# Batch 0's second part in nine transfers to tiles of their own, and two more raw buffers for the first sixteen weight loads

## The chip, the cores and the metric

The kernel runs on one core of one Trainium2 chip. The metric is the device time of one execution in microseconds. Five engines work in parallel, each through its own instructions in a fixed order: PE (matmul, with PEld for its weight loads), DVE, ACT and POOL (elementwise work), and SP, which here only issues DMA transfers. Who must wait for whom is settled by semaphores.

## The reference

Three layers follow one another. In the attention, for each of 4 batches and 8 heads (576 rows, 64 columns), a causal softmax of q and k is applied to v, and mixed with a memory read-out.

```python
scores = np.where(causal, -1000000000.0, scale * q @ k.T)
a = softmax(scores); local = a @ v
mem_out = (phi(q) @ M_prev) / (phi(q) @ z_prev + 1e-6)      # phi(x) = elu(x) + 1
attn = g * mem_out + (1 - g) * local                         # g = sigmoid(beta) by head
h = x @ moe_w_in;  y = (h * sigmoid(h)) @ moe_w_out          # 512 -> 2048 -> 512
g = y @ w_gate;    out = (silu(g) * (y @ w_val)) @ w_out     # 512 -> 1536 -> 512
```

## The kernel before

The weights are 64-bit numbers, so each tile of them is loaded as raw integers (`raw8`, 512 KB), decoded to float32 by ACT (L731) and DVE (L732, L733), and split by ACT and POOL (L214, L773) into a high and a low half, `w`. The attention works on pairs of heads. Batch 0 is done in two parts: part A takes rows 0 to 255 for all four pairs (phase "A"), part B rows 256 to 575 (phase "B"); the later batches follow pair by pair. As soon as part A is done, the first MoE layer starts on it: matmuls `h` (L870) with four raw tiles of the first weights, the gate (`th`, `gh`, `gl`), then matmuls `y` (L928) with four raw tiles of the second weights. The layer is cut into four weight slices, in the order `A0 A1 B1 B0 A2 B2 A3 B3` of part and slice; `w` tiles are also stored to DRAM (`wd`, L796) and fetched again later. A generator interleaves MoE matmuls and attention steps, and a scheduler then fixes each engine's order before the program runs, by times that it estimates. What stands in an engine's order is not changed by the hardware.

One pair of part B is this chain: transposes of q and k (`psq`, `psk`, L367), evacuation to `Q` and `kT` on ACT (L220), six score products (`pss`, L434 and L509), each with a minimum on DVE (L486, L510), five exponentials on ACT, the normalisation (`r` on DVE, `s` on POOL, L523), transposes of the result (`pst`), their evacuation (`tb`), and the product with v (`U`, L619), which gives `x` for the MoE layer. The memory read-out runs beside it (`e`, `qp`, `psm`, `n`, `mr`). The attention's products share five PSUM banks, so PE can start the next product only when DVE or ACT has emptied a bank.

In part B each pair's rows are loaded into one `q_t` and one `k_t` and one of two `v_t`; the next pair's q and k follow when the transposes of this pair are through (`lq`), and v when the pair is done (`lv`). `Prep` holds the raw weight tiles: three buffers, loaded two ahead:

```python
            self.done[key] = self.split(t, key)
            self.prefetch(ahead)
            for d, t in self.post:
                nc.sync.dma_start(out=d, in_=t)
```

Of the kernel before, what the change touches and what calls it, by code (L numbers as in the profile page):

```python
# [8 lines left out]
F32 = mybir.dt.float32  # L9
# [4 lines left out]
I32 = mybir.dt.int32  # L14
# [3 lines left out]
P = 128  # L18
BIG = 1.0e9
CFG = dict(  # L20
    raw8=3,
    raw=3,
    g=1,
    th=2,
    ps_m=3,
    ps_a=dict(A=5, B=5, G=5),
    ps_s=dict(),
    run=3000,
# [3 lines left out]
    rows=1,  # L32
# [14 lines left out]
    ahead=2,  # L47
# [18 lines left out]
    n_rows=2,  # L66
    n_s4=dict(A=0, B=2, F=2, G=1),
    lb=3,
    bufsA={'*': 4},
    bufsB={'*': 2},  # L70
    bufsF={'*': 2},
# [22 lines left out]
def kernel(  # L94
# [15 lines left out]
    nc = tc.nc  # L110
    B, H, S, D = q.shape
# [4 lines left out]
    NP = H // 2  # L116
    NT = B * S
    SA = 256
# [10 lines left out]
    def f(ap):  # L129
        return ap.bitcast(F32)  # L130
# [20 lines left out]
    kp = kept.enter_context(tc.tile_pool(name="kp", bufs=1))  # L151
    pha = ExitStack()
    rawp = pha.enter_context(tc.tile_pool(name="rawp", bufs=CFG["raw"], side="right"))
    cur, ph2 = {"raw": rawp}, {}
# [72 lines left out]
    rows, bds = {}, []  # L227
# [14 lines left out]
            q4s.append(t)  # L242

    q4s, gate = [], []
    rowsA = {}
    units = []

    def bd_of(u):
# [3 lines left out]
    def load_bd(b, eng):  # L252
        t = bds[b % 2]
        for hh in range(2):
            r = slice(64 * hh, 64 * hh + 64)
            eng.dma_start(
                out=t[r, :, 64 * hh:64 * hh + 64], in_=M_prev[b].rearrange("(p c) d e -> c d p e", c=2)[hh]
            )
            with nc.allow_non_contiguous_dma(reason="one number of each row"):
                eng.dma_start(out=t[r, :, P + hh], in_=z_prev[b].rearrange("(p c) d -> c d p", c=2)[hh])  # L260

    def load_A():
        for nm in "qkv":
            rowsA[nm] = cur["pool"].tile([P, 2, H, D], F32, name=nm + "A")

        def go(nm, h, eng):
            src = {"q": q, "k": k, "v": v}[nm]
            for c in range(2):
                eng.dma_start(
                    out=rowsA[nm][:, c, h], in_=src[0, h, P * c:P * c + P, :].rearrange("h p d -> p h d")  # L270
                )

        go("q", slice(0, 2), nc.sync)
        go("k", slice(0, 2), nc.scalar)
        go("q", slice(2, 4), nc.sync)
        go("k", slice(2, 4), nc.scalar)
        go("q", slice(4, 8), nc.sync)
        go("k", slice(4, 8), nc.sync)
        nc.sync.dma_start(out=bt, in_=beta.rearrange("(o h) -> o h", o=1).broadcast_to([P, H]))
        load_bd(0, nc.sync)  # L280
        go("v", slice(0, 8), nc.sync)

    owner = {}

    def rows_of(u):
        return rows[u % len(rows)]

    def load_rows(u, names):
        b, p, sups = units[u]
        t = rows_of(u)  # L290
        for nm in names:
            owner[nm, u % len(rows) if nm == "v" else 0] = u
            src = {"q": q, "k": k, "v": v}[nm]
            c0 = 0 if nm == "v" or 0 in sups else 2
            for hh in range(2):
                x = src[b, 2 * p + hh]
                nc.sync.dma_start(
                    out=t[nm][:, c0:4, hh, :], in_=x[P * c0:512, :].rearrange("(c p) d -> p c d", p=P)
                )
            x = src[b, 2 * p:2 * p + 2]  # L300
            if nm == "v":
                nc.sync.dma_start(out=t[nm][0:64, 4], in_=x[:, 512:S].rearrange("h p d -> p h d"))
            else:
                nc.sync.dma_start(out=t[nm][:, 4], in_=x[:, S - P:S].rearrange("h p d -> p h d"))
# [41 lines left out]
    def unit(u):  # L346
        b, p, sups = units[u]
        o = {}
        ph = "A" if sups == (0,) else "B" if sups == (1,) else "F" if b < CFG["stackb"] else "G"
# [4 lines left out]
        hs2 = slice(2 * p, 2 * p + 2)  # L354
# [2 lines left out]
            return CFG.get(ph, {}).get(key, CFG[key])  # L357

        def own(nm):
            assert ph == "A" or owner[nm, u % len(rows) if nm == "v" else 0] == u, (nm, u)  # L360

        def row_of(nm, c):
            return rowsA[nm][:, c, hs2] if ph == "A" else rows_of(u)[nm][:, c]

        def T(dst, src, start=True):
            n = src.shape[0]
# [2 lines left out]
        def transposed(nm, sup, out, e, scale):  # L369

            own(nm)
            ps = cur["ps_a"].tile([P, 512], F32, tag="a", name="ps" + nm)
            n = (SA, SB)[sup]
            for i, c in enumerate(BLK[sup]):
                x = P * i if c < 4 else n - P
                T(ps[:, x:x + P], row_of(nm, c).rearrange("p h d -> p (h d)"))
            cps(e, out, ps[:, 0:n], scale)
# [215 lines left out]

        def AV():
            own("v")
            Us = {}
            for sup in sups[::-1]:
# [32 lines left out]

        def nxt_load(names):
            w = u + (len(rows) if names == "v" else 1)
            if ph != "A" and w < len(units) and w >= NP:
                load_rows(w, names)

        def nxt_bd():
# [39 lines left out]
    slots, ready, at_slot = {}, {}, 0  # L676
    for u, key in enumerate(units):
        step, stages = unit(u)
# [14 lines left out]
    NSLOT = max(slots) + 1  # L693

    def load_B():
        for u in range(NP, NP + len(rows)):
            load_rows(u, "qkv" if u == NP else "v")

    slots[1].insert(0, setup_beta)
    slots[CFG["lb"]].append(load_B)  # L700
    slots[CFG["lb"]].append(lambda: load_bd(1, nc.sync))

    def attn_slot(s):
        for st in slots[s]:
# [2 lines left out]

    w1 = {}

    def load64(w, j, part, after=None):  # L710

        raw = cur["raw"].tile([P, 512, 2], I32, tag="raw8", name="raw8", bufs=CFG["raw8"])
        w2 = w.bitcast(I32)
        if after is not None:
            nc.gpsimd.tensor_copy(raw.bitcast(F32)[:, 0, 0:1], f(after))
        if part == 0:
            nc.sync.dma_start(
                out=raw.rearrange("p (k n) t -> p k (n t)", k=KD),
                in_=w2[:, 2 * P * j:2 * P * (j + 1)].rearrange("(k p) n -> p k n", p=P),
            )  # L720
        else:
            nc.sync.dma_start(out=raw.rearrange("p n t -> p (n t)"), in_=w2[P * j:P * j + P, :])
        return raw

    def decode(raw, t=None):
        hi, lo = raw[:, :, 1], raw[:, :, 0]
        u = hi.bitcast(F32)
        if t is None:
            t = cur["raw"].tile([P, 512], F32, tag="raw", name="raw", bufs=CFG["raw"])
        ti = t.bitcast(I32)  # L730
        nc.scalar.activation(out=t, in_=u, func=ACTF.Prelu, scale=2.0**-111, alpha=-(2.0**32))  # L731
        nc.vector.tensor_single_scalar(ti, ti, 3, op=ALU.logical_shift_left)  # L732
        nc.vector.scalar_tensor_tensor(ti, lo, 29, ti, ALU.logical_shift_right, ALU.bitwise_or)  # L733
        return t

    seen = {}

    def r_(ap):
        return ap.bitcast(F32R)

    def raw_w1(*key):
        if key in seen:
            return None
        if key[0] == 0:
            return load64(w1_in, key[1], 0)
        raw = cur["raw"].tile([P, 512, 2], I32, tag="raw8", name="raw8", bufs=CFG["raw8"])
        _, s, e = key
        nc.sync.dma_start(
            out=raw.rearrange("p (j n) t -> p j (n t)", j=NW),
            in_=w1_out.bitcast(I32)[P * NW * s:P * NW * (s + 1), 2 * P * e:2 * P * (e + 1)].rearrange(  # L750
                "(j p) n -> p j n", p=P
            ),
        )
        return raw

    def split_w1(t, key):
        if key in seen:
            w = wp.tile([P, 2, 512], F32, tag="w", name="w")
            nc.sync.dma_start(out=w, in_=seen[key])
            return r_(w[:, 0]), r_(w[:, 1])  # L760
        w = split_wp(decode(t), "1")
        seen[key] = dram.tile([P, 2, 512], F32, name="wd%d_%d" % (key[0], len(seen)))
        prep1.post.append((seen[key], w))
        return r_(w[:, 0]), r_(w[:, 1])

    def split_wp(t, kind):
        w = wp.tile([P, 2, 512], F32, tag="w", name="w")
        split_to(r_(w[:, 0]), r_(w[:, 1]), t, kind)
        return w
# [5 lines left out]
    class Prep:  # L775
# [9 lines left out]
                key = self.todo.pop(0)  # L785
                self.raws.append((key, self.load(*key)))

        def step(self, ahead=CFG["ahead"]):
            self.prefetch(1)
            if not self.raws:  # L790
                return
            key, t = self.raws.pop(0)
            self.done[key] = self.split(t, key)
            self.prefetch(ahead)
            for d, t in self.post:
                nc.sync.dma_start(out=d, in_=t)  # L796
            self.post = []

        def need(self, key):
            while key not in self.done:  # L800
# [3 lines left out]


    prep1 = Prep(raw_w1, split_w1)

    def token_block(key):
# [594 lines left out]
    if True:  # L1403
        open_at("atA")
        setup_attn()
        load_A()
        setup()
        items = moe1()
# [7 lines left out]
        for sg in segs:  # L1416
            r = sg["r"]
# [5 lines left out]
        for kind, val in items:  # L1423
# [7 lines left out]
            else:  # L1431
# [3 lines left out]
                if goals:  # L1435
                    x = (cost - c0) / (goals[0][0] - c0)
# [20 lines left out]
        with tc.manual_schedule(engines={mybir.EngineType.PE}):  # L1457
            for n, (kind, i, x, y) in enumerate(pos):
# [3 lines left out]
                else:  # L1462
                    down(i, x, y)
                    k = x * NJ2 + y
# [38 lines left out]
```

## Time and profile before

| what | value |
|---|---|
| median of 3 runs | 1058.24 us (1055.73 to 1062.23) |
| the profiled execution | 1061.61 us, its span 1059.8 us |
| PE busy | 1035.1 us (98% of the span) |
| DVE, ACT, POOL busy | 647.3, 539.8, 394.6 us |
| granted TensorE clock, mean | 0.993 |
| bytes moved by DMA | 258.16 MB, mean 244 GB/s |

The span runs from the first to the last instruction; the profiled execution's own time is 1.8 us more. Busy shares are means over stages with different limits: from 660 us on PE alone sets the time, and the change stands in the first 110 us.

### The profile page before, as it was taken

The numbers are of one execution on the slowest core, as the hardware profiler recorded it, in microseconds if no ns is written. First come the engines' busy times: TensorE is split into PE (matmuls) and PEld (weight loads), VectorE is DVE, ScalarE is ACT, GpSimd is POOL, SyncE is SP. The second block draws the span as 40 slices with busy tenths as digits, with TensorE's granted clock in tenths as the row PEclk, the third lists the DMA queues.
The fourth block names the chain that finished last, engine by engine and source line by source line (L and its number), as shares of the span: only waits on it lengthen the run. The fifth ranks groups of instructions, "written<-read, shape, count | busy, mean of one in ns | idle before, by whom it ended". The sixth has DMA issues, their size and how long they took to land.

```text
span 1059.8 us, 18826 instructions
## 1 busy us (share of the span) xinstructions
PE 1035.1 (98%) x6622; PEld 953.2 (90%) x6622; DVE 647.3 (61%) x1521; ACT 539.8 (51%) x1259; POOL 394.6 (37%) x463
## 2 busy tenths in 40 slices
PE   7799999999999999999999999999999999999998
PEld 5577988888878899888999899999999999999998
DVE  6796767886545644765245553566845669356573
ACT  6684877866656655675454441333613336133351
POOL 4684644678656647552579651000000000000000
PEclk9899999999999999999999999999999999999999
DMA  8995766478977569762299866777987778777784
GB/s 195 321 301 156 253 222 200 119 236 266 297 254 260 183 203 365 254 200 74 100 313 308 336 238 229 251 258 249 339 261 265 250 250 285 255 268 246 250 286 147
DMA packets 168670, 258.16 MB, mean 244 GB/s; under 512 B 76800, under 2 KB 113152, under 8 KB 168576
## 3 DMA queue, kind: packets, MB, share of 16 engines
q1 hardware_dynamic: 167488, 256.70, 73.3%
q8 instruction: 53, 0.87, 0.3%
q10 hardware_dynamic: 1088, 0.26, 0.1%
q14 instruction: 41, 0.34, 0.1%
HBM read 197.67 MB, written 59.24 MB: 242 GB/s over the span
## 4 chain that ended last, share of the span: by engine, by line
PE 79%; DVE 6%; POOL 4%; DMA 4%; ACT 4%; issue 3%; SPq 0%; POOLq 0%; ACTq 0%; DVEq 0%
PE y L928 14%; PE h L870 13%; PE oac L1207 11%; PE gb L1207 11%; PE po L1314 9%; PE pb L1314 4%; PE U L619 4%; PE gd L1207 4%; PE pss L434 3%; PE pst L367 3%; PE psm L445 1%; DMA raw<-in_moe_w_out_dram 1%; DMA raw<-in_moe_w_gate_dram 1%; POOL wo L996 1%; DVE raw L733 1%
## 5 line engine op out<-in xcount | busy, mean ns | idle before, releaser
L870 PE MATMUL h<-x,w 128*128 128x432 f32 (+2 forms) x1152 | 226.4, 346 | 4.4 <-ACT w L214 3.0
L870 PEld LDWEIGHTS h<-x,w 128*128 128x128 f32 x1152 | 196.6, 190 | 16.5 <-ACT w L214 3.2
L928 PE MATMUL y<-gh,w 128*128 128x432 f32 (+2 forms) x768 | 166.3, 349 | 2.7 <-DVE th L878 1.6
L928 PEld LDWEIGHTS y<-gh,w 128*128 128x128 f32 x768 | 131.6, 190 | 14.5 <-issue 3.5
L880 POOL TENSOR_TENSOR gl<-th,gh 128x432 fp32r<-128x432 f32 (+2 forms) x96 | 105.5, 1102 | 78.7 <-ACT gh L214 63.9
L1207 PE MATMUL gb<-yT,w 128*128 128x384 f32 x648 | 124.8, 336 | 0.0
L1207 PEld LDWEIGHTS gb<-yT,w 128*128 128x128 f32 x648 | 113.1, 188 | 0.0
L878 DVE SCALAR_TENSOR_TENSOR th<-th,h 128x432 f32<-128x432 f32 (+2 forms) x96 | 52.5, 550 | 80.7 <-ACT th L877 80.6
L523 POOL TENSOR_TENSOR s<-s,r 128x128 f32<-128x128 f32 (+4 forms) x96 | 68.4, 740 | 74.5 <-DVE r L540 19.8
L1314 PE MATMUL po<-w,ph 128*128 128x256 f32 x516 | 93.8, 283 | 0.0
L928 PE MATMUL y<-gl,w 128*128 128x432 f32 (+2 forms) x384 | 88.5, 344 | 0.6 <-POOL gl L880 0.6
L490 ACT ACTIVATE s<-s,mn 128x128 f32<-128x128 f32 (+3 forms) x128 | 70.9, 555 | 22.6 <-DVE mn L486 21.2
L1207 PE MATMUL oac<-yB,w 128*128 128x384 f32 x432 | 81.3, 336 | 0.0
L1314 PEld LDWEIGHTS po<-w,ph 128*128 128x128 f32 x516 | 81.2, 191 | 0.0
L732 DVE TENSOR_SCALAR raw<-raw 128x512 int32<-128x512 int32 x68 | 42.0, 618 | 62.6 <-ACT raw L731 62.3
L1279 ACT CAST ph<-r 128x384 fp32r<-128x384 f32 x108 | 51.0, 513 | 56.0 <-DVE r L1233 35.7
L1207 PEld LDWEIGHTS oac<-yB,w 128*128 128x128 f32 x432 | 75.4, 188 | 0.0
L1314 PE MATMUL po<-w,pl 128*128 128x256 f32 x258 | 73.0, 283 | 0.0
L928 PEld LDWEIGHTS y<-gl,w 128*128 128x128 f32 x384 | 67.6, 190 | 4.3 <-POOL gl L880 1.5
L214 ACT CAST gh<-th 128x432 fp32r<-128x432 f32 (+2 forms) x96 | 49.1, 513 | 42.8 <-DVE th L878 31.5
L731 ACT ACTIVATE raw<-raw 128x512 f32<-128x512 f32 x68 | 45.5, 669 | 48.1 <-DMA raw<-in_moe_w_gate_dram 17.3
L1280 DVE TENSOR_TENSOR pl<-r,ph 128x384 fp32r<-128x384 f32 x108 | 55.9, 554 | 17.8 <-ACT ph L1279 17.1
(163 smaller groups left out, 1999.5 us busy)
## 6 DMA issues: line engine op xcount, KB each, us to landing
w<-wg SPq DMA_DIRECT2D x108, 512.0 KB, 4.7
w<-wd SPq DMA_DIRECT2D x80, 512.0 KB, 5.5
wg<-wo SPq DMA_DIRECT2D x36, 512.0 KB, 3.6
w<-woT SPq DMA_DIRECT2D x36, 512.0 KB, 4.9
wd<-w SPq DMA_DIRECT2D x32, 512.0 KB, 4.2
raw<-in_moe_w_out_dram SPq DMA_DIRECT2D x28, 512.0 KB, 5.5
w<-woB SPq DMA_DIRECT2D x27, 512.0 KB, 4.8
w<-wg SPq DMA_DIRECT2D x36, 256.0 KB, 4.8
```

Source lines behind the costliest of these rows:

```text
L214: nc.scalar.copy(out, in_)
L490: nc.scalar.activation(out=a, in_=a, func=ACTF.Exp, scale=-1.0, bias=mn, accum_out=o["sm", sup][:, col:col + 1])
L523: nc.gpsimd.tensor_mul(a, a, r.to_broadcast([P, w]))
L731: nc.scalar.activation(out=t, in_=u, func=ACTF.Prelu, scale=2.0**-111, alpha=-(2.0**32))
L870: nc.tensor.matmul(ps[:, :nt], w[:, kk, :], x[:, kk, :nt], start=(m == 0), stop=(m == 3 * KD - 1))
L878: nc.vector.scalar_tensor_tensor(th[:, :nt], th[:, :nt], 1.0, ps[:, :nt], ALU.add, ALU.mult)
L880: tt(CFG["gl" if n >= CFG["n0"] else "gl0"]).tensor_sub(gl[:, :nt], th[:, :nt], f(gh[:, :nt]))
L928: nc.tensor.matmul(ps[:, :nt], w[:, c], g[:, :nt], start=(m == 0), stop=(m == last))
L1207: nc.tensor.matmul(dst, w[wi][:, P * kk:P * kk + P], y[ny][:, yi, kk], start=(start and m == 0), stop=(stop and m == 5), skip_group_check= ...
L1279: nc.scalar.copy(ph, src)
L1280: nc.vector.tensor_sub(pl, src, f(ph))
L1314: nc.tensor.matmul(dst, a[:, c], x, start=(begin and m == 0 and own_bank), stop=(end and m == 2), skip_group_check=True,)
```

## The change

Rows 256 to 575 of q, k and v of batch 0 are loaded for all four pairs at once, by three transfers each, into `qB`, `kB` and `vB`, which nothing overwrites. The first two row blocks of v come from part A's `vA`, which now lives on through part B. So phase B has no row loads of its own, and the loads of batch 1's first pair have nothing to wait for. Of the first sixteen raw tiles, numbers 2, 4, 7, 9, 12 and 14 come from two extra buffers, and until sixteen are loaded the queue runs four ahead in place of two. The store of a `w` tile is issued one step later (`hold`). The memory matrix of batch 1 is asked for at step 14 in place of step 3 (`lb1`).

```diff
+    lb1=14,
+    hold=1,
+    early=16,
...
-            rowsA[nm] = cur["pool"].tile([P, 2, H, D], F32, name=nm + "A")
+            rowsA[nm] = (kp if nm == "v" else cur["pool"]).tile([P, 2, H, D], F32, name=nm + "A")
...
         def row_of(nm, c):
-            return rowsA[nm][:, c, hs2] if ph == "A" else rows_of(u)[nm][:, c]
+            if ph in "AB":
+                return rowsA[nm][:, c, hs2] if c < 2 else rowsB[nm][:, c - 2, hs2]
+            return rows_of(u)[nm][:, c]
...
         def nxt_load(names):
             w = u + (len(rows) if names == "v" else 1)
-            if ph != "A" and w < len(units) and w >= NP:
+            if 2 * NP <= w < len(units):
                 load_rows(w, names)
...
     def load_B():
-        for u in range(NP, NP + len(rows)):
-            load_rows(u, "qkv" if u == NP else "v")
+        for nm in "qkv":
+            t = rowsB[nm] = kp.tile([P, 3, H, D], F32, name=nm + "B")
+            x = dict(q=q, k=k, v=v)[nm][0]
+            if nm == "v":
+                nc.gpsimd.memset(t[64:128, 2], 0.0)
+            for c in range(2):
+                nc.sync.dma_start(out=t[:, c], in_=x[:, SA + P * c:SA + P * c + P, :].rearrange("h p d -> p h d"))
+            r = slice(512, S) if nm == "v" else slice(S - P, S)
+            nc.sync.dma_start(out=t[0:64, 2] if nm == "v" else t[:, 2], in_=x[:, r, :].rearrange("h p d -> p h d"))
...
+    def raw_tile():
+        n_raw[0] += 1
+        if n_raw[0] <= CFG["early"] and n_raw[0] % 5 in (2, 4):
+            return kp.tile([P, 512, 2], I32, tag="raw8", name="raw8", bufs=2)
+        return cur["raw"].tile([P, 512, 2], I32, tag="raw8", name="raw8", bufs=CFG["raw8"])
...
-        def step(self, ahead=CFG["ahead"]):
+        def step(self):
+            ahead = 4 if n_raw[0] < CFG["early"] else CFG["ahead"]
...
-            for d, t in self.post:
-                nc.sync.dma_start(out=d, in_=t)
-            self.post = []
+            while len(self.post) > CFG["hold"]:
+                self.store()
```

The scheduler gives other orders from about the first 12 us on; they are the same again, instruction by instruction, from PE's 1875th of 6257 on. The line numbers of the changed kernel are higher (L372 is L367, L439 is L434, L514 is L509, L491 is L486, L753 is L733). Three places show what moved.

On SP before, behind the third raw weight tile (`raw_156` is the first): the rows of pair 0, in twelve transfers with v of pair 1, stand ahead of the fourth raw tile.

```order
L717 DMA raw_168<-in_moe_w_in_dram 128x4x256
L297 DMA q_t_98<-in_q_dram 128x2x64 x2
L304 DMA q_t_98<-in_q_dram 128x2x64
L297 DMA k_t_99<-in_k_dram 128x2x64 x2
L304 DMA k_t_99<-in_k_dram 128x2x64
L297 DMA v_t_100<-in_v_dram 128x4x64 x2
L302 DMA v_t_100<-in_v_dram 64x2x64
L297 DMA v_t_102<-in_v_dram 128x4x64 x2
L302 DMA v_t_102<-in_v_dram 64x2x64
L717 DMA raw_194<-in_moe_w_in_dram 128x4x256
```

And now, from the same raw tile on:

```order
L737 DMA raw_168<-in_moe_w_in_dram 128x4x256
L737 DMA raw_170<-in_moe_w_in_dram 128x4x256
L768 DMA raw_172<-in_moe_w_out_dram 128x4x256
L707 DMA qB<-in_q_dram 128x8x64 x2
L709 DMA qB<-in_q_dram 128x8x64
L707 DMA kB<-in_k_dram 128x8x64 x2
L709 DMA kB<-in_k_dram 128x8x64
L707 DMA vB<-in_v_dram 128x8x64 x2
L709 DMA vB<-in_v_dram 64x8x64
L259 DMA bd_106<-in_M_prev_dram 64x4x64
L768 DMA raw_197<-in_moe_w_out_dram 128x4x256
```

Raw tiles four and five moved ahead of the rows, the rows of all pairs stand in one run, and the memory matrix of batch 1 (`bd_106`) stands right behind them, as it did.

On PE before, in part B, from the last score product of pair 0 to that of pair 1:

```order
L509 MATMUL pss_670<-kT_151,q_108 128x320
L367 MATMUL psq<-ident,q_t_98 128x128 x3
L870 MATMUL h<-x,w 128x256 x4
L367 MATMUL psk<-ident,k_t_99 128x128 x2
L445 MATMUL psm<-bd_104,qp 128x130 x3
L367 MATMUL psk<-ident,k_t_99 128x128
L870 MATMUL h<-x,w 128x256 x8
L434 MATMUL pss<-kT_181,Q 128x384 x2
L434 MATMUL pss<-kT_181,Q 128x512 x2
L870 MATMUL h<-x,w 128x256 x4
L928 MATMUL y<-gh,w 128x256 x8
L928 MATMUL y<-gl,w 128x256 x3
```

And now, from the same product on:

```order
L514 MATMUL pss_666<-kT_151,q_108 128x320
L372 MATMUL psq<-ident,qB 128x128 x3
L372 MATMUL psk<-ident,kB 128x128 x3
L450 MATMUL psm<-bd_104,qp 128x130 x3
L439 MATMUL pss<-kT_184,Q 128x384 x2
L439 MATMUL pss<-kT_184,Q 128x512 x2
L514 MATMUL pss_791<-kT_184,q_110 128x256
L514 MATMUL pss_794<-kT_184,q_110 128x320
L372 MATMUL psq<-ident,qB 128x128 x3
L372 MATMUL psk<-ident,kB 128x128 x3
L450 MATMUL psm<-bd_104,qp 128x130 x3
```

The MoE matmuls between are gone: the first four of the second slice now stand behind 19 transposes of pair 0 and the first two score products of pair 2.

On DVE before, from the last score minimum of pair 0 on:

```order
L510 ISA s_581,mn_666<-pss_670,mask_65 128x320
L510 ISA mn_666 128x1
L733 SCALAR_TENSOR_TENSOR raw<-raw_416,raw 128x512
L515 TENSOR_TENSOR mn_644<-mn_666 128x1
L732 TENSOR_SCALAR raw<-raw 128x512
L733 SCALAR_TENSOR_TENSOR raw<-raw_629,raw 128x512
L533 TENSOR_SCALAR r_782<-sm_645 128x5
L534 RECIPROCAL r_782<-r_782 128x5
L535 TENSOR_TENSOR r_782<-r_782,omg 128x4
```

And now (`raw_245` is the seventh raw tile, where `raw_629` is the ninth):

```order
L515 ISA s_577,mn_662<-pss_666,mask_65 128x320
L515 ISA mn_662 128x1
L520 TENSOR_TENSOR mn_640<-mn_662 128x1
L752 TENSOR_SCALAR raw<-raw 128x512
L454 TENSOR_SCALAR n_717<-psm 128x6
L409 TENSOR_SCALAR e<-Q 128x320
L753 SCALAR_TENSOR_TENSOR raw<-raw_245,raw 128x512
L455 RECIPROCAL n_717<-n_717 128x6
L456 TENSOR_TENSOR n_717<-n_717,g_bc 128x6
L458 MEMSET n_717 64x2
L460 TENSOR_TENSOR mr_722<-psm,n_717 128x384
L538 TENSOR_SCALAR r_770<-sm_641 128x5
```

By the normalisation (L533, now L538) nine raw tiles had been decoded, and now seven; the read-out of pair 0 and the phi of pair 1 stand ahead of the normalisation of pair 0.

## Rows read from the trace of the kernel before

**Rows 1.** Busy time by stage: stretch, length, busy us (instructions), TensorE clock, DMA share, GB/s
```profile
0.00:85.00 85.00, 71.77 (x421) 52.11 (x422) 69.37 (x209) 58.97 (x159) 57.96 (x75) 0.94 0.91 269
85.00:110.00 25.00, 25.00 (x200) 20.21 (x198) 12.82 (x39) 10.40 (x29) 6.59 (x7) 1.00 0.45 127
110.00:240.00 130.00, 129.98 (x993) 115.96 (x992) 98.81 (x296) 101.11 (x264) 79.35 (x94) 1.00 0.66 209
240.00:350.00 110.00, 104.62 (x646) 90.99 (x645) 64.71 (x174) 68.57 (x169) 73.13 (x89) 0.98 0.83 272
```

**Rows 2.** The chain that ended last, 0 to 130 us: start, length, piece
```profile
26.51 6.95 DMA raw<-in_moe_w_out_dram
...
52.77 3.70 DMA k_t<-in_k_dram
...
100.59 1.42 PE y L928 x12
...
110.20 7.04 PE h L870 x48
```

**Rows 3.** What PE waited for, 0 to 110 us: total, times, longest
```profile
PE psq L367 <- POOL ident masks.py:199: 3.2, 1, 3.2
PE h L870 <- ACT w L214: 3.0, 1, 3.0
...
PE psq L367 <- DMA q_t<-in_q_dram: 1.7, 2, 0.9
```

**Rows 4.** Busy time by stage inside the attention of batch 0's second part
```profile
39.00:68.00 29.00, 23.43 (x138) 17.91 (x134) 27.18 (x70) 21.43 (x54) 24.36 (x25) 0.88 0.98 311
68.00:85.00 17.00, 16.19 (x101) 11.12 (x102) 15.64 (x39) 12.06 (x32) 13.47 (x14) 1.00 0.90 271
...
46.00:48.00 2.00, 0.00 (x0) 0.00 (x0) 1.46 (x3) 2.00 (x7) 1.23 (x1) 0.50 0.84 270
```

**Rows 5.** Groups on DVE, 30 to 110 us: form, count, busy, mean ns, idle before
```profile
L733 DVE SCALAR_TENSOR_TENSOR raw<-raw,raw 128x512 int32<-128x512 int32 x15 | 13.3, 885 | 0.2
L732 DVE TENSOR_SCALAR raw<-raw 128x512 int32<-128x512 int32 x15 | 8.6, 574 | 2.5 <-ACT raw L731 2.4
...
L486 DVE CUSTOM_DVE_ANT_0 s<-pss,mask 128x512 f32<-128x512 f32 x8 | 5.3, 682 | 0.6 <-PE pss L434 0.6
L486 DVE CUSTOM_DVE_ANT_0 s<-pss,mask 128x384 f32<-128x384 f32 x8 | 4.2, 548 | 0.0
...
L451 DVE TENSOR_TENSOR n<-n,g_bc 128x6 f32<-128x6 f32 x4 | 3.1, 782 | 0.0
L406 DVE SCALAR_TENSOR_TENSOR qp<-Q,e 128x320 f32<-128x320 f32 x4 | 3.1, 776 | 0.7 <-ACT e L405 0.7
```

**Rows 6.** The weights' raw tiles, 9 to 110 us: duration ns min/median/max, first, last
```profile
L733 DVE SCALAR_TENSOR_TENSOR raw<-raw,raw x19: 679/693/1556, 17.4 to 90.0; 128x512 int32<-128x512 int32 x19
```

**Rows 7.** PE in order of time: start, length, instructions
```profile
38.64 1.77 PE L434 MATMUL pss<-kT,Q 64*128 64x384 f32 x8
...
73.44 0.49 PE L367 MATMUL psq<-ident,q_t 128*128 128x128 f32 x3
...
74.99 2.28 PE L619 MATMUL U<-tb,v_t 128*64 128x192 f32 x20
...
78.36 1.04 PE L367 MATMUL pst<-ident,s 128*128 128x128 f32 x8
79.16 1.50 PE L870 MATMUL h<-x,w 128*128 128x256 f32 x10
...
87.33 1.24 PE L509 MATMUL pss<-kT,q 128*128 128x256 f32 x4
```

**Rows 8.** What the DMA queue on SP waited for, 0 to 200 us
```profile
SPq L796 <- POOL w L773: 40.8, 20, 6.6
```

**Rows 9.** DMA issues, 9 to 40 us: count, KB each, median us to landing
```profile
vA<-in_v_dram SPq DMA_DIRECT2D x2, 256.0 KB, 3.8
...
q_t<-in_q_dram SPq DMA_DIRECT2D x6, 64.0 KB, 5.8
```

More of the change, by code (lines that the diff above doesn't have):

```diff
@@ L244 @@
     q4s, gate = [], []
-    rowsA = {}
+    rowsA, rowsB = {}, {}
     units = []
@@ L359, in own @@
         def own(nm):
-            assert ph == "A" or owner[nm, u % len(rows) if nm == "v" else 0] == u, (nm, u)
+            assert ph in "AB" or owner[nm, u % len(rows) if nm == "v" else 0] == u, (nm, u)
         def row_of(nm, c):
-            return rowsA[nm][:, c, hs2] if ph == "A" else rows_of(u)[nm][:, c]
+            if ph in "AB":
+                return rowsA[nm][:, c, hs2] if c < 2 else rowsB[nm][:, c - 2, hs2]
+            return rows_of(u)[nm][:, c]
         def T(dst, src, start=True):
@@ L695, in load_B @@
     def load_B():
-        for u in range(NP, NP + len(rows)):
-            load_rows(u, "qkv" if u == NP else "v")
+        for nm in "qkv":
[7 more added lines that the diff above has]
+            nc.sync.dma_start(out=t[0:64, 2] if nm == "v" else t[:, 2], in_=x[:, r, :].rearrange("h p d -> p h d"))
     slots[1].insert(0, setup_beta)
     slots[CFG["lb"]].append(load_B)
-    slots[CFG["lb"]].append(lambda: load_bd(1, nc.sync))
+    slots[CFG["lb1"]].append(lambda: load_bd(1, nc.sync))
     def attn_slot(s):
@@ L708 @@
     w1 = {}
+    n_raw = [0]
+    def raw_tile():
[3 more added lines that the diff above has]
+        return cur["raw"].tile([P, 512, 2], I32, tag="raw8", name="raw8", bufs=CFG["raw8"])
     def load64(w, j, part, after=None):
-        raw = cur["raw"].tile([P, 512, 2], I32, tag="raw8", name="raw8", bufs=CFG["raw8"])
+        raw = raw_tile()
         w2 = w.bitcast(I32)
@@ L745, in raw_w1 @@
             return load64(w1_in, key[1], 0)
-        raw = cur["raw"].tile([P, 512, 2], I32, tag="raw8", name="raw8", bufs=CFG["raw8"])
+        raw = raw_tile()
         _, s, e = key
@@ L758, in split_w1 @@
             w = wp.tile([P, 2, 512], F32, tag="w", name="w")
+            prep1.stored(key)
             nc.sync.dma_start(out=w, in_=seen[key])
@@ L762, in split_w1 @@
         seen[key] = dram.tile([P, 2, 512], F32, name="wd%d_%d" % (key[0], len(seen)))
-        prep1.post.append((seen[key], w))
+        prep1.post.append((key, w))
         return r_(w[:, 0]), r_(w[:, 1])
@@ L794, in step, with store, stored @@
             self.prefetch(ahead)
-            for d, t in self.post:
-                nc.sync.dma_start(out=d, in_=t)
-            self.post = []
+            while len(self.post) > CFG["hold"]:
+                self.store()
+        def store(self):
+            key, w = self.post.pop(0)
+            nc.sync.dma_start(out=seen[key], in_=w)
+        def stored(self, key):
+            while key in [x for x, _ in self.post]:
+                self.store()
         def need(self, key):
```

## The prediction

> **What bounds the kernel now.** I read the busy time by stage first. From 110 to 240 us PE is busy 129.98 of 130 us at full clock; between 240 and 350 us it stands for 5.4 us [rows 1], and behind that it is nearly always busy (98% of the span in all). So an edit to the first 110 us can give only what PE loses there: 13.2 us idle up to 85 us, 3.2 of them at the start before the identity is built [rows 3], plus the slow clock, 0.94 in the mean [rows 1]. From 39 to 68 us PE runs at 0.88, and within 46 to 48 us, after a gap, at 0.50, which is the 1.2 GHz level [rows 4]. At that level a busy microsecond does half a microsecond's work; the loss up to 85 us is at most 0.06 of 85, that is 5 us, and less where PE stood idle anyway. The ceiling of a gain is so 10.0 + 5 = 15 us.
>
> Then I asked who makes PE wait. The chain of waits names DMA: a raw tile of the second weights for 6.95 us and rows of k for 3.70 us [rows 2]. But PE itself stood only 1.7 us for rows of q, and 3.0 us for a weight tile on ACT [rows 3]. In the same stretch DVE is busy 27.18 of 29 us [rows 4]. That decides my reading: **DVE sets the pace from 39 to 85 us**, and DMA, though as busy (0.98), is late by little. From 85 us on DVE has half its time free and PE a backlog.
>
> **The change part by part.** I sum to one place that both orders pass with the same work done, the **hand-over**: part B's attention is through, 24 `h` matmuls of 320 columns and the ten transposes of batch 1's first pair too. Before, that is at 110.20 us, where 48 `h` matmuls begin [rows 2].
>
> *Loads.* Nine transfers take the place of 36, and v's first 256 rows are not fetched twice: 0.5 MB less. The transfers of a pair no longer queue behind stores of weights, for which SP waited 40.8 us in all [rows 8]; `hold` moves each store one step later, past the next raw load. Against that, batch 1's first q, k and two v now come early, 1.3 MB into the busiest stretch. Counting SP's order up to the ninth raw tile gives 7.7 MB before and 8.5 MB now; at 311 GB/s [rows 4] that tile lands 2.5 us later, but DVE now reaches it some 10 us later (below), so it is hidden; were that cover gone, 2.5 us would show. What is won on PE is the wait for q, 1.7 us; the 3.0 us wait for a weight tile goes from its place too, since the matmul that waited moves. The memset of `vB` stands ahead of the identity on POOL; PE's second transpose waits for q's transfer at that time, so I price it between 0 and 0.5 us and take 0. The memory matrix of batch 1 keeps its place on SP: 0.
>
> *Two more raw buffers, four ahead.* Raw tiles four and five land before the rows. The x of part A hangs on POOL and PE, and the first 39 us stay as they are: 0, within 0.5 us either way.
>
> *The order.* This is the dear part. In PE's new order, between the first slice's `h` and the transposes of k for pair 3, there stand only attention and 12 `h`: three sets of four score products at 1.77, three pairs of L509 at 1.24, 18 transposes of q and k at 0.16, six read-outs (as a transpose) 0.8, 19 transposes of the result at 0.13, 12 `h` at 0.15 [rows 7]: 5.3 + 3.7 + 2.9 + 0.8 + 2.5 + 1.8 = **17 us of PE work**. PE cannot run through them, since each product waits for a bank that DVE empties. DVE's queue to the same place, by its order: five decodes at 0.885 + 0.574, six minima of 512 columns at 0.682 and six of 384 at 0.548, two `qp` at 0.776, two long `n` at 0.782 [rows 5]: 7.3 + 4.1 + 3.3 + 1.6 + 1.6 = 17.9; and an estimate for the rest from the nearest rows: two `e` as `qp` 1.6, two `tb` and two `mr` as the minima 2.5, six shorter minima at 0.5, 3.0, and a gate, the small steps of `r` and the accumulator reads, 4: 11. Together **29 us**. It starts with the first minimum, 0.9 us after the products of pair 0 begin at 38.64 [rows 7]: the place is reached at **68.5 us**, with 12 us of PE idle or slow in 29, where before PE lost 29 - 23.43 = 5.6 idle and 0.12 x 29 = 3.5 at the most by its clock [rows 4].
>
> What is then left to the hand-over: four U with their transposes at 2.28 + 0.4 = 10.7; 36 `h` at 0.15 = 5.4; 96 `y` at 1.42/12 [rows 2] = 11.4; 57 transposes at 0.13 = 7.4; read-outs 0.8; pair 3's scores 1.8 + 1.2; 24 `h` at 7.04/48 [rows 2] = 3.5; ten transposes 1.3: **43.5 us**. DVE is ahead of PE there: pair 3's minima, some 12 us behind, fall before PE asks for the last of them. Hand-over 68.5 + 43.5 = 112.0, **1.8 us later**. The same prices on the old order from 68 us on give 40.5 where the trace has 41.4 without its 0.8 idle [rows 4], so they are good to 1 us.
>
> *How fast DVE is.* L733 takes 0.68 us at the least and 1.56 at the most [rows 6], and its mean of 0.885 is made beside POOL's work. Five decodes at their floor would save 5 x 0.2 = 1.0, and the long `n`, `e` and `qp`, if they shrank by a third, some 1.5 more: the hand-over 0.7 us early. The other end is that all of DVE's long operations meet POOL: five decodes at 1.56 in place of 0.885, 3.4 us later. The Trainium skill (GPSIMD Engine Reference, 1. Specifications) says that GpSimd's SBUF interfaces are shared with VectorE, and that instructions with two SBUF inputs contend; the trace agrees, L733 having two and a spread of 0.68 to 1.56.
>
> *After the hand-over* PE is full to 240 us, so a delay goes through. The 5.4 us that PE stands from 240 to 350 us follow raw loads and POOL; they may swallow all of it or none. I take half: 0.9 us remain. On the profiled execution's 1061.61 that is 1062.5; this execution lies 3.4 us above the median of 1058.24, so against the median **1059.1, say 1059**. Its own range: DVE's ends -0.7 and +5.2, and 3 us either way for the stretch up to 297 us, whose order also changes and in which I price no wait: 1054 to 1066.
>
> **The rivals.**
>
> *A. DMA was the bound.* For it: the chain's two DMA pieces, 6.95 + 3.70 = 10.65 us [rows 2], and a DMA share of 0.98 at 311 GB/s [rows 4]. Against it: PE's own wait for DMA is 1.7 us, and DVE has no room for more than 1.8 of 29 us. If the pieces go wholly: 1058.2 - 10.7 = 1047.6; if DVE is next after 4 us: 1054. Centre 1050. The rows' merging could help by itself: a transfer of 256 KB lands in 3.8 us, one of 64 KB in 5.8 [rows 9]. The Trainium skill (DMA: Bandwidth & Descriptors, Specifications) wants pieces of at least 512 B for line rate and so speaks against that gain: the rows stay 64 numbers, 256 B; by that rule the merging gives nothing of its own, and A comes out at no better than its 1054. No run here parts the two.
>
> *B. PE falls to the low clock in the thin stretch, and becomes the bound itself: slower.* Before, a gap of some 5 us ended in 0.50 [rows 4]. Now 17 us of work lie thinly in 29. At half speed they take 34, 5 us more than DVE gives; with the 1.8 of above and nothing swallowed later 1058.2 + 6.8 = 1065, and with DVE's slow end 1068. It decides if PE's clock lies below 17/29 = 0.59 in the mean of that stretch. Against it: before, the clock was 0.88 there.
>
> *C. The loads move and nothing else does:* the rows were hidden and the order evens out by the hand-over, as DVE's total work is the same in both. Time: 1058.
>
> **How the numbers follow.** Forecast 0.52, A 0.20, B 0.16, C 0.12. A change of 1% is 10.6 us, about what a measurement of this kernel tells from none. Faster by more needs A in full: 0.10 with a little for the stretch behind; slower by more needs B with the slow end of DVE: 0.09; the rest, 0.81, lies within. The likeliest is 1059. The range reaches down into A's lower half, 1048, and over B's centre, 1067.
>
> **What would show it.** In the changed kernel's profile: no wait of PE on `qB` or `kB`; transposes of q for pair 3 at 65 to 70 us where they were at 73.44 [rows 7]; PE busy near 17 us between 39 and 68 us in place of 23.4, DVE again over 26; the hand-over between 109 and 116 us. PE's clock between 45 and 65 us parts B from the rest. I am wrong if DVE's busy share there falls clearly, which would say that DMA had held it; if the 19 transposes wait for POOL's scaling; or if PE's waits between 240 and 300 us change by more than 3 us, from the new order there.

## The result, and the profile after

The changed kernel takes 1064.84 us (median of 14 executions, 1061.62 to 1070.41) where the kernel before takes 1058.36 (14 executions, 1055.73 to 1064.55). The ratio is 1.0060, with a 95% interval of 1.0044 to 1.0076: **slower by 6.5 us, 0.6%**. That lies in the stated range and within 1%, but well above the likeliest 1059.

The first two profiled executions don't show it: both spans are 1059.8 us, since the one of before lies 3 us above its median and the one of the changed kernel 3 us below. So both kernels were run again; those two profiles have spans of 1056.9 (before) and 1061.8 us (changed), and they are the ones read below. In the changed kernel, busy time by stage, the answer to [rows 1]:

```profile
0.00:85.00 85.00, 71.60 (x413) 50.04 (x415) 66.12 (x209) 57.62 (x156) 54.37 (x73) 0.94 0.81 242
85.00:110.00 25.00, 24.46 (x201) 20.73 (x198) 16.45 (x41) 13.76 (x35) 10.86 (x13) 1.00 0.69 222
110.00:240.00 130.00, 128.75 (x962) 112.69 (x961) 102.23 (x290) 96.90 (x253) 77.23 (x89) 1.00 0.64 199
240.00:350.00 110.00, 107.22 (x680) 94.00 (x679) 66.86 (x180) 71.06 (x174) 75.69 (x92) 1.00 0.84 275
```

By this view hardly anything is lost: PE is as busy as before up to 85 us, 1.8 us less busy from 85 to 240 us, and busier from 240 to 350 us. The loss appears only when both kernels are compared at places where they have done the same work. Each engine's order is fixed, so one can list the places up to which both orders hold the same set of matmuls, and read from the timeline when the next one starts:

| matmuls done | before, us | changed, us | later by | in the first pair of profiles |
|---|---|---|---|---|
| 502, the hand-over | 109.89 | 110.97 | 1.08 | 0.76 |
| 862 | 162.84 | 164.06 | 1.22 | 0.89 |
| 1004 | 183.02 | 185.90 | 2.88 | 2.57 |
| 1123 | 199.52 | 203.61 | 4.09 | 3.77 |
| 1345 | 231.92 | 236.90 | 4.98 | 4.65 |
| 1444 | 246.39 | 254.35 | **7.96** | **7.62** |
| 1611 | 279.14 | 283.94 | 4.80 | 4.15 |
| 1873, orders equal from here | 325.72 | 330.14 | 4.42 | 1.30 |

Up to the hand-over 1.1 us are lost, about what was forecast. **The next 6.9 us go between 110 and 254 us, where PE was thought full**, and 3.5 come back behind that. The first pair of profiles agrees to 0.35 us up to the 1444th matmul; behind it the first execution of before stood longer (from 240 to 350 us 5.4 us in [rows 1], 3.7 in the second profile), which hid the loss.

Inside the attention of part B (changed kernel, busy time by stage; the last row is the stretch of the sum, from the first scores of pair 0 to the transposes of k for pair 3), the answer to [rows 4]:

```profile
39.00:50.00 11.00, 9.05 (x38) 4.72 (x37) 10.20 (x37) 10.00 (x26) 6.24 (x8) 0.84 1.09 338
50.00:60.00 10.00, 6.13 (x34) 4.16 (x33) 9.87 (x25) 7.48 (x17) 8.50 (x9) 0.94 1.02 348
60.00:68.00 8.00, 8.00 (x52) 6.24 (x51) 5.74 (x19) 5.00 (x14) 6.75 (x7) 0.86 0.62 227
...
38.77:65.19 26.42, 20.60 (x96) 12.81 (x95) 24.02 (x72) 20.06 (x50) 18.91 (x21) 0.87 0.97 325
```

What PE waited for up to 112 us (changed kernel), the answer to [rows 3]:

```profile
PE psq L372 <- POOL ident masks.py:199: 3.8, 1, 3.8
PE pss L439 <- DVE mn L491: 3.0, 1, 3.0
PE pst L372 <- POOL s L528: 2.1, 3, 1.3
PE pss L439 <- ACT kT L223: 1.2, 1, 1.2
PE psm L450 <- DVE mn L491: 1.1, 2, 0.8
```

And three rows of PE's timeline (changed kernel), the answer to [rows 7]: the transposes of q and k for pair 3, and the hand-over.

```profile
63.90 0.49 PE L372 MATMUL psq<-ident,qB 128*128 128x128 f32 x3
...
65.19 0.49 PE L372 MATMUL psk<-ident,kB 128*128 128x128 f32 x3
...
110.97 2.22 PE L899 MATMUL h<-x,w 128*128 128x320 f32 x14
```

Two more answers. DVE, 30 to 110 us (count, busy, mean ns), to [rows 5], and SP's wait for POOL, to [rows 8]:

```profile
L753 DVE SCALAR_TENSOR_TENSOR raw<-raw,raw 128x512 int32<-128x512 int32 x14 | 13.3, 948 | 0.1
...
L411 DVE SCALAR_TENSOR_TENSOR qp<-Q,e 128x320 f32<-128x320 f32 x4 | 2.3, 570 | 0.2 <-ACT e L410 0.2
...
L456 DVE TENSOR_TENSOR n<-n,g_bc 128x6 f32<-128x6 f32 x4 | 1.1, 264 | 0.1
```

```profile
SPq L822 <- POOL w L794: 33.0, 15, 5.4
```

DVE is busy 20.1 of 21 us between 39 and 60 us, and PE's waits there name DVE's minima (`mn`). There is no wait for `qB`, `kB` or a weight tile. The identity comes 0.6 us later, behind the memset of `vB`; after seven matmuls 0.1 of it is left, since PE waits for q's rows there anyway.

### The profile page after: what moved, and what is told of

Its sections match the earlier page's. It is cut to its first block, busy times and chain, and to the rows that moved or that the text cites. A ratio compares the mean times of both kernels' runs of the same rounds, so it can differ in the third digit from the quotient of the medians.

```text
span 1059.8 us, 18772 instructions
## 1 busy us (share of the span) xinstructions
PE 1036.5 (98%) x6622; PEld 953.7 (90%) x6622; DVE 653.0 (62%) x1521; ACT 540.5 (51%) x1259; POOL 396.7 (37%) x464
## 4 chain that ended last, share of the span: by engine, by line
PE 78%; DVE 9%; DMA 5%; ACT 4%; issue 3%; POOL 2%; SPq 0%; ACTq 0%; POOLq 0%; DVEq 0%
PE y L957 14%; PE h L899 13%; PE oac L1236 11%; PE gb L1236 11%; PE po L1343 9%; PE pb L1343 4%; PE gd L1236 4%; PE pss L439 3%; PE U L624 3%; PE pst L372 3%; DVE raw L753 2%; DMA woT<-wo 1%; PE psm L450 1%; DVE raw L752 1%; DMA ytop<-yd 1%
## 5 line engine op out<-in xcount | busy, mean ns | idle before, releaser
L957 PE MATMUL y<-gh,w 128*128 128x432 f32 (+2 forms) x768 | 162.7, 346 | 1.1 <-DVE yp L962 0.5
L491 DVE CUSTOM_DVE_ANT_0 s<-pss,mask 128x128 f32<-128x128 f32 (+3 forms) x128 | 58.3, 483 | 14.9 <-PE pss L439 14.4
```

The lines of the kernel that those rows point to most:

```text
L491: nc.vector.tensor_tensor_reduce(out=a, in0=at[i](hh), in1=mask[:, 512 - w:512], op0=ALU.add, op1=ALU.min, scale=1.0, scalar=3.0e38, accum ...
L957: nc.tensor.matmul(ps[:, :nt], w[:, c], g[:, :nt], start=(m == 0), stop=(m == last))
```

## The experiments

Ratios are to the kernel before, run on the same chip in the same rounds.

**Both kernels once more**, unchanged.

> The kernel before, unchanged, for the bound of the measurement and for the granted clock of each of its timed executions; the profiles of the first pair show equal spans (1059.8 us), though the medians are 6.5 us apart. Both theories: ratio 1.000, between 0.998 and 1.002, median near 1058.4. Theory 'waits' (the new order makes PE stand or wait longer at the same clock): mean clock of the executions as for the changed kernel, 0.993 to 0.995, and at one clock the changed kernel 5 to 7 us longer. Theory 'clock' (PE falls to the low level more often): mean clock higher by 0.004 to 0.006, that is 0.998 to 0.999, and at one clock the two kernels equal.

> The changed kernel, unchanged, for a second profile: the first profiled execution (1061.79 us) was 3 us below its median. Both theories: 1062 to 1066 us, ratio 1.004 to 1.008. Theory 'waits': between 85 and 350 us PE stands 5 to 7 us longer than before. Theory 'clock': the same idle time, and the granted clock lower in one stage, where before had 1.00. The hand-over at 110 to 113 us by both.

Before: ratio 1.0000 (0.9988 to 1.0012), so 1.3 us is what this comparison can part. Changed: 1064.94 us, 1.0055 (1.0041 to 1.0070). The granted clock is 0.995 in both profiles, with spans 4.9 us apart, and over the timed executions its mean is 0.994 for both kernels: the theory "clock" falls. "Waits" falls too in the form that was written down: between 85 and 350 us PE stood 4.57 us (0.54 + 1.25 + 2.78, from the rows above) where before's second profile has 3.69, all of it in one row, so the idle time grew by 0.9 us and not by 5 to 7.

```profile
240.00:350.00 110.00, 106.31 (x667) 92.42 (x667) 68.88 (x185) 71.89 (x177) 75.44 (x91) 1.00 0.83 277
```

**The two parts apart.** Rows alone (first diff), and buffers alone (second, against before):

```diff
-    lb1=14,
-    hold=1,
-    early=16,
+    lb1=3,
+    hold=0,
+    early=0,
```

```diff
+    early=16,
...
+        if n_raw[0] <= CFG["early"] and n_raw[0] % 5 in (2, 4):
+            return kp.tile([P, 512, 2], I32, tag="raw8", name="raw8", bufs=2)
...
+            ahead = 4 if n_raw[0] < CFG["early"] else CFG["ahead"]
```

> The nine transfers and the tiles of their own alone, with three raw buffers and two ahead as before. Its engine orders are those of the changed kernel from PE's 429th instruction on. Theory 'order' (what costs is the order that these loads set free, up to PE's 1875th instruction): all of it stays, 1063 to 1066 us, ratio 1.005 to 1.008. Theory 'buffers' (what costs is four raw tiles ahead, which crowd the DMA and DVE at the start): 1057 to 1060 us, ratio 0.999 to 1.002.

> The two extra raw buffers and four ahead alone; part B's rows pair by pair as before. Theory 'order': 1057 to 1060 us, ratio 0.999 to 1.002, although this alters PE's order too. Theory 'buffers': 1063 to 1066 us, ratio 1.005 to 1.008. If both parts cost only together, both this and the other part alone lie within 0.999 to 1.002.

Rows alone: 1064.90 us, 1.0052 (1.0038 to 1.0066). Buffers alone: 1066.61 us, 1.0070 (1.0055 to 1.0085). Neither theory foresaw that each part alone costs as much as both together. The two costs differ in kind. With rows alone the table above repeats: 0.70 us late at the hand-over, 7.65 after 1444 matmuls. With buffers alone 9 us are lost before 110 us. Two more raw tiles stand ahead of the rows there, which still come pair by pair, and the chain that ended last runs through transfers of `k_t` for 5.75, 1.72 and 2.84 us between 40 and 78 us; that this is the cause is read from the chain and not tested. PE's waits and its clock there (buffers alone):

```profile
PE pst L370 <- ACT Q L223: 4.3, 1, 4.3
PE pss L437 <- ACT kT L223: 4.0, 1, 4.0
```

```profile
68.00:85.00 17.00, 8.72 (x38) 5.75 (x37) 14.29 (x32) 10.19 (x27) 12.10 (x12) 0.70 0.78 252
```

Beside the nine transfers the buffers cost nothing that these runs can part: the two together are no worse than the rows alone. `hold` taken back leaves every engine's order as it is, and without the buffers `lb1` too, so neither was run by itself.

**Loads against order.** The orders of PE, DVE and ACT of one kernel were tied onto the other by edges that fix only the order of issue, and make nothing wait for an end (`places` is the order of the other kernel, written as a table):

```diff
+        for a, b in zip(places, places[1:]):
+            tc.add_manual_dep(
+                mine[b],
+                mine[a].name,
+                _mybir_.DependencyInfo(_mybir_.DependencyClass.NoSync, _mybir_.DependencyReason.DATA),
+                reason="replay",
+            )
...
         tile_attention_moe_moe_kernel(tc, *args)
+        _replay(tc)
```

> All of the change's transfers and buffers, but the instructions of PE, DVE and ACT are tied to the order that the kernel before has; POOL's and SP's come out nearly so by themselves. Theory 'order' (the change's cost is the order that it sets free): 1056 to 1060 us, ratio 0.998 to 1.001. Theory 'loads' (it is the transfers themselves, where they lie and what they meet): 1063 to 1066 us, ratio 1.005 to 1.008.

> The kernel before with its own transfers and buffers, but with PE, DVE and ACT tied to the changed kernel's order. Theory 'order': 1063 to 1068 us, ratio 1.004 to 1.009 (up to 2 us more than the changed kernel, since rows that this order wants early still come late). Theory 'loads': 1057 to 1060 us, ratio 0.999 to 1.002.

New loads in the old order: 1063.08 us, 1.0034 (1.0022 to 1.0046), between the theories. It arises ahead of the hand-over: 4.39 us late there, and still 4.36 after 1444 matmuls. One wait makes it (PE's waits, then ACT's, 38 to 56 us):

```profile
PE h L899 <- ACT w L217: 7.5, 1, 7.5
```

```profile
ACT raw L751 <- DMA raw<-in_moe_w_in_dram: 3.3, 2, 2.4
```

In [rows 3] the same wait is 3.0 us. The raw tiles behind it come later: rows of all pairs and batch 1's first loads stand ahead of the ninth, which lands at 47.4 us where it was 41.5. Old loads in the new order: 1070.78 us, 1.0100 (1.0081 to 1.0120), above both theories; 9.84 us late at the hand-over, since this order asks early for rows that come late, and 7.05 more up to the 1444th matmul, as in the changed kernel. So loads and order belong together ahead of 110 us, and behind it, up to the 1444th matmul, the order alone decides.

**The order behind the hand-over alone**, the same edges on PE only and from the 504th matmul on (shown is the first line of PE's table of positions, as it was for the whole order and as it is now):

```diff
-        '0 2 1 3+2 6 5 8+3 7 11+4 16+2 15 18+41 61 88 106 59+2 64+6 130 62+2 89 107 131 70 73 76+8 71+2 74+2 '
+        '503+23 538+12 556+12 580+2 526+12 550 552 554 582+10 603+3 551 553 555 606 568 570 572 569 571 '
```

> The changed kernel, with PE tied to the order of before from its 504th instruction on, the hand-over; ahead of that everything as in the changed kernel. In the second pair of profiles the changed kernel is 1.1 us late at the hand-over and 4.4 us at PE's 1873rd instruction. Theory 'order, behind the hand-over': only the first 1.1 us stay, 1059 to 1060.5 us, ratio 1.000 to 1.002. Theory 'order, ahead of it' or 'loads': 1063 to 1066 us, ratio 1.004 to 1.008.

> The kernel before, with PE tied to the changed kernel's order from its 504th instruction on alone. Theory 'order, behind the hand-over': it pays the 3.3 us that the changed kernel lost there and nothing else, 1060.5 to 1062.5 us, ratio 1.002 to 1.004. Theory 'loads', or 'order, ahead of the hand-over': 1057 to 1060 us, ratio 0.999 to 1.001.

The changed kernel with the old order from there: 1062.37 us, 1.0017 (1.0002 to 1.0032). The kernel before with the new order from there: 1062.87 us, 1.0029 (1.0018 to 1.0040). Both ratios are as the first theory said; in microseconds the medians are 1.9 and 0.4 us above its bounds, and the kernel before was 1059.69 here. In the profiles, the lateness against before's second profile (the profiled execution of the first kernel lies 3.2 us below its median):

| matmuls done | changed, old order from there | before, new order from there |
|---|---|---|
| 502 | 2.62 | 0.59 |
| 1004 | 2.57 | 3.51 |
| 1444 | 2.52 | 8.59 |
| 1611 | 1.77 | 5.48 |
| 1873 | 1.73 | 5.11 |

The old order loses 0.1 us or less from 502 to 1444 in every run that has it, whatever the loads; the new one 6.9 to 8.0. This settles that **the order behind the hand-over, set by PE's,** is the cause of the larger part. With PE's order tied, the scheduler gave DVE and ACT nearly the other kernel's order behind the hand-over too (38 and 25 positions differ from before in the first, 10 and 6 from the changed kernel in the second), so PE's order is not parted from theirs.

**What in that order costs.** The two stretches of equal work, busy time by stage, kernel before and changed:

```profile
109.89:246.39 136.50, 136.50 (x1036) 122.16 (x1035) 105.57 (x304) 107.62 (x280) 85.97 (x101) 1.00 0.68 214
```

```profile
110.97:254.35 143.38, 140.53 (x1036) 123.81 (x1034) 110.37 (x303) 106.10 (x274) 88.84 (x102) 1.00 0.65 200
```

Of 6.88 us PE stands idle for 2.85; for 4.03 it is busy longer over the same matmuls, at the same clock. The 120 score products of the later batches hold 1.9 of that (16.6 us in place of 14.7), other matmuls the rest. The timeline shows how the score products come by theirs. The score products of a pair of heads contract over 64 rows each. Kernel before, the block of 384 columns, both heads side by side:

```profile
169.13 0.45 PE L434 MATMUL pss<-Kl,Qh 64*128 64x384 f32 x2
169.41 0.34 PE L434 MATMUL pss<-Kh,Qh 64*128 64x384 f32 x2
169.58 0.35 PE L434 MATMUL pss<-Kh,Ql 64*128 64x384 f32 x2
169.86 0.66 PE L367 MATMUL U<-ident,mr 128*128 128x128 f32 x4
```

Changed kernel, the same block:

```profile
167.90 0.44 PE L439 MATMUL pss<-Kl,Qh 64*128 64x384 f32 x1
168.18 0.33 PE L439 MATMUL pss<-Kh,Qh 64*128 64x384 f32 x1
168.36 0.34 PE L439 MATMUL pss<-Kh,Ql 64*128 64x384 f32 x1
168.62 0.55 PE L899 MATMUL h<-x,w 128*128 128x320 f32 x2
169.10 0.44 PE L439 MATMUL pss<-Kl,Qh 64*128 64x384 f32 x1
169.38 0.33 PE L439 MATMUL pss<-Kh,Qh 64*128 64x384 f32 x1
169.56 0.33 PE L439 MATMUL pss<-Kh,Ql 64*128 64x384 f32 x1
169.82 0.55 PE L372 MATMUL U<-ident,mr 128*128 128x128 f32 x3
```

From 169.13 to 169.86 six products take 0.73 us; from 167.90 to 168.62 three take 0.72, and the other three the same again. Two heads side by side cost as much as one alone. The Trainium skill (TensorEngine Tiling (Array Packing), Key Properties) says that tiles of 64 rows work in parallel and that a change of tiling mode drains the engine; the first agrees with 0.73 against 0.72. The second would fit the two `h` between, which take 0.48 us (168.62 to 169.10) where two in a long row take 0.29 (7.04/48 each in [rows 2]), but no run here measures it by itself. Between the 502nd and the 1444th matmul the heads stand apart in six places now, and in three before. The last experiment puts them together, by the same edges on PE: in all eleven places of the changed kernel's order and all nine of the other. One of them (PE's order, changed kernel):

```diff
-L899 MATMUL h<-x,w 128x320 x13
-L439 MATMUL pss<-Kl,Qh 128x384
-L439 MATMUL pss<-Kh,Qh 128x384
-L439 MATMUL pss<-Kh,Ql 128x384
-L899 MATMUL h<-x,w 128x320 x2
-L439 MATMUL pss<-Kl,Qh 128x384
-L439 MATMUL pss<-Kh,Qh 128x384
-L439 MATMUL pss<-Kh,Ql 128x384
+L899 MATMUL h<-x,w 128x320 x15
+L439 MATMUL pss<-Kl,Qh 128x384 x2
+L439 MATMUL pss<-Kh,Qh 128x384 x2
+L439 MATMUL pss<-Kh,Ql 128x384 x2
```

> The kernel before, with one thing altered in PE's order: the score products of the two heads of a pair (three of 64 rows for each head), which stand apart in nine places with other work between, are put side by side, where the second head's stand. By the trace two heads side by side take 0.71 us for 384 columns and apart 2 x 0.72; 0.50 and 2 x 0.56 for 256. Theory 'apart costs': nine places at some 0.65 less, up to 5 us where PE is full: 1054 to 1057 us, ratio 0.995 to 0.998. Theory 'filler' (a place that is given up costs as much as it saves, since PE waits for the second bank or DVE comes later): 1058 to 1061 us, ratio 0.999 to 1.002.

> The changed kernel with the same alteration: eleven places, six of them ahead of PE's 1445th instruction, where before had three. Of the 6.9 us that the changed kernel loses there the pairs apart would be 2.0 by the sum of the score products' times (16.5 against 14.6 us). Theory 'apart costs': 1058 to 1062 us, ratio 0.999 to 1.003 (eleven places at 0.65 below 1064.9). Theory 'waits' (PE's waits for DVE and ACT are all of it): 1063 to 1066 us, ratio 1.004 to 1.007.

Changed kernel, joined: 1060.03 us, 1.0012 (0.9995 to 1.0029), where it was 1.0055: 4.6 us won by this edit, as the theory "apart costs" said, and no longer to be told from before. (DVE and ACT follow here too, from 118 us on: 156 and 113 positions of their orders change.) Kernel before, joined: 1057.21 us, 0.9978 (0.9965 to 0.9991), **faster than both kernels**, by 2.3 us, at the near end of what that theory said in ratio; this is two fifths of what nine places at 0.65 would give, and no run shows where the rest went.

So the kernel before pays for heads apart as well. With both joined, the change still costs some 3 us (1060.03 against 1057.21 us on one chip; the intervals of the two ratios do not overlap): heads apart account for about half of its 6.5 us. Between the 502nd and the 1444th matmul 2.4 of the 6.9 us remain (changed, joined, and before, joined):

```profile
113.90:252.72 138.82, 137.03 (x1035) 121.52 (x1033) 107.06 (x302) 105.65 (x272) 88.30 (x101) 1.00 0.67 206
```

```profile
110.33:246.71 136.38, 135.16 (x1037) 120.85 (x1035) 106.60 (x304) 107.13 (x278) 86.81 (x101) 1.00 0.68 213
```

In the profile of the joined changed kernel the lateness from the 502nd to the 1508th matmul is 1.8 us where it was 5.9. Up to the 1444th PE is busy 3.5 us less than unjoined, 2.6 of it in the score products (14.0 us where they took 16.6), and stands 1.8 us in place of 2.85. Its waits, from 110 to 335 us, changed kernel and then joined:

```profile
PE h L899 <- DVE th L907: 1.6, 1, 1.6
PE pst L372 <- ACT Q L223: 1.0, 1, 1.0
```

```profile
PE pst L372 <- ACT Q L223: 0.7, 1, 0.7
...
PE h L899 <- DVE th L907: 0.4, 1, 0.4
```

Against the kernel before as it was, the joined one loses 2.3 us up to the 1444th matmul: it stands 1.8 us, in small waits for DVE and ACT, and is busy 0.5 us longer. No run takes this apart further.

## Why the prediction was right and wrong

**DVE sets the pace from 39 to 85 us: right up to 60 us, wrong behind that.** DVE is busy 20.1 of 21 us there and PE's waits name its minima. From 60 to 68 us PE is never idle and DVE busy 5.74 of 8. DMA is only just behind DVE: in the old order the same loads make ACT and PE wait for a raw tile. The sentence that its delay of 2.5 us would show "were that cover gone" was sound: the ninth raw tile lands at 45.2 us where it was 41.5, 3.7 us later, unseen; in the old order, which has no cover, 4.4 us show at the hand-over. That `hold` moves each store past the next raw load was wrong, since it alters no order.

**The sum to the hand-over: right within its own error, by two errors that cancel.** Pair 3's transposes of k were put at 68.5 us and stand at 65.19: from the first minimum (39.7 us) the 29 us came out as 25.5. The prices held in sum, but adding them did not give the time. The durations of DVE's 70 instructions there sum to 28.2 us, yet the next one starts some 0.08 us before the last has ended, and the accumulator reads start together with their follower, so together they fill 23.5 us; DVE stood for the other 2.0. Adding durations put 4.7 us too many on DVE, and the sum had no idle time. The rest up to the hand-over took 45.8 us in place of 43.5. That they cancel in part is luck: 110.97 against 112.0. Before, the hand-over is at 109.95 us in the timeline (109.89 in the second profile); 110.20 is where the chain's piece begins. So the forecast delay was rather 2.1 us, and 1.1 were measured. "PE busy near 17" between 39 and 68 us was wrong, as 9.05 + 6.13 + 8.00 = 23.18 there: the place came earlier, so 2.8 us of full work stand behind it, and slow matmuls count as busy; from 38.77 to 65.19 it is 20.60 at a clock of 0.87, which is 17.9 at full clock.

**The step that failed** is "*After the hand-over* PE is full to 240 us, so a delay goes through", with a new order "in which I price no wait" and 3 us either way. A different order in a stretch where PE is 99.98% busy was taken to cost nothing on the mean. It cost 6.9 us. Side by side or apart could be counted in the two orders, and six places against three with the time of a single product would have given some 2 us; the waits that came with them no row of before shows. The sign that was to catch this, PE's waits between 240 and 300 us, looked elsewhere: PE stood 2.8 us there where before has 3.3 and 3.7, since the loss lies ahead of 254 us and is more busy time than idle.

**Why the number still lay in the range** is luck for the larger part. The room above 1059 was made of 3.4 us for DVE's slow end and of rival B, and neither came: L753's mean is 0.948 us, not 1.56. With the 3 us for the order alone the range would have ended at 1062, and 1064.84 lies above that.

**The swallowing** was sized at half of the delay of 1.8 us and was larger: 3.5 us came back behind the 1444th matmul. From there to the 1873rd before stands 3.7 us and the changed kernel 1.2; the other 1.0 is less busy time. PE's own waits there name ACT and DVE (before, second profile, from 110 to 335 us), where the prediction named raw loads and POOL:

```profile
PE pst L367 <- ACT Q L220: 1.4, 1, 1.4
PE psk L367 <- DVE mr L455: 1.4, 1, 1.4
```

Less these 3.5, 1.1 + 6.9 ends as 4.4 in this pair of profiles, and 4.9 at the end of the span. The medians are 6.5 us apart; of the 1.6 us between, 1.3 is how far this profiled execution (1063.68 us) lies below its kernel's median, and no profile places the rest.

**The rivals.** A (DMA) gives no gain, as forecast, though its reading of the loads holds in the old order. B (the low clock) is at work in some executions and doesn't decide: its condition, below 0.59 in the thin stretch, is not met at 0.87. With the same order ahead of the hand-over the clock from 60 to 68 us was 0.86 in the changed kernel, 0.78 with the old order tied on behind, and 0.64 joined, and the hand-over 1.1, 2.6 and 4.0 us late (1.3 of the last arise before 34 us; from 26 to 31 us its clock is 0.50 where the changed kernel's was 0.79). The last two kernels, busy time by stage:

```profile
60.00:68.00 8.00, 8.00 (x47) 5.85 (x46) 5.45 (x17) 3.76 (x11) 6.74 (x7) 0.78 0.49 183
```

```profile
60.00:68.00 8.00, 8.00 (x34) 5.32 (x33) 5.38 (x18) 3.32 (x9) 5.42 (x7) 0.64 0.50 186
```

C (nothing else moves) falls with the table. The other signs of being wrong did not show: DVE is busy 25.8 of 29 us from 39 to 68 us (forecast over 26), and the waits for POOL's scaling, 2.1 us, lie before 25 us.

## What to carry to other kernels

A change to loads under a scheduler is a change of order, and the order far behind the loads may cost more than the place that was edited; compare two traces where both have done the same set of matmuls, not at equal times, since busy shares hide it. Before pricing a new order at nothing, count in it the pairs of 64-row products that no longer stand side by side. Do not add up an engine's instruction durations to a time before looking whether they overlap. Profile each kernel more than once when single executions scatter by as much as the effect.

## What the runs showed of the hardware

PE's busy share doesn't tell how much it does: 136.50 us of work took 140.53 busy microseconds at a granted clock of 1.00.

Durations on DVE overlap in the profile: 70 instructions of 28.2 us in sum filled 23.5 us (changed kernel, from 39.67 to 65.19 us).

The same DVE instruction takes longer in the new order though its own work is the same. The mean of the difference `Ql` of batches 1 and later, from 110 to 335 us, is 0.70 to 0.75 us in the four profiles with the old order there and 1.26 to 1.33 in the five with the changed kernel's. Before and changed:

```profile
L415 DVE TENSOR_TENSOR Ql<-Q,Qh 128x512 fp32r<-128x512 f32 x8 | 5.6, 704 | 1.1 <-ACT Qh L414 1.1
```

```profile
L420 DVE TENSOR_TENSOR Ql<-Q,Qh 128x512 fp32r<-128x512 f32 x8 | 10.4, 1299 | 1.0 <-ACT Qh L419 0.9
```

The order in time of DVE and POOL settles which of them last long. Changed kernel, POOL then DVE; then before, DVE first:

```profile
159.66 1.67 POOL L794 TENSOR_TENSOR w<-raw,w 128x512 fp32r<-128x512 f32 x1 [0.80 <-POOL q L219]
160.09 1.78 DVE L420 TENSOR_TENSOR Ql<-Q,Qh 128x512 fp32r<-128x512 f32 x1
```

```profile
161.28 0.68 DVE L415 TENSOR_TENSOR Ql<-Q,Qh 128x512 fp32r<-128x512 f32 x1
161.76 1.34 POOL L415 TENSOR_TENSOR Kl<-K,Kh 128x512 fp32r<-128x512 f32 x1 [1.44 <-ACT Kh L414]
```

In the first, `w` ends at 161.33 us and `Ql` 0.54 us behind it. So it is in all twelve profiles: a `Ql` that begins while POOL runs no instruction takes 0.67 to 0.69 us (24 of them), even where POOL begins one beside it; one that begins while POOL runs an instruction ends no earlier than 0.54 us behind that one's end (70 of them), and six in the changed kernel last 1.1 to 1.8 us by this. So which of the two begins first decides, and the new order alters that. In the stretch of 143.38 us DVE is 4.8 us busier than before, about what eight `Ql` at 1.30 in place of 0.70 add; whether PE's waits for DVE come from it, no run shows.
